# Split-product scores for the later pairs, first loads ahead of the branch, and a changed last sum and last stores in an attention and two-MLP kernel

## Chip, cores and metric

The kernel runs on one core of one Trainium2 chip. The metric is device microseconds of that core for one launch. Five engines run side by side, each through its own queue of instructions in order: PE (TensorE, matrix products; its weight loads are listed as PEld), DVE (VectorE), ACT (ScalarE), POOL (GpSimd) and SP (SyncE, which only issues DMAs here). They wait for one another through semaphores.

## Reference

```python
def _attn_ref(q, k, v, cap):                 # q, k, v: 4 x 12 x 448 x 64, cap = 30
    scores = scale * np.matmul(q, k.transpose(0, 1, 3, 2))
    scores = cap * np.tanh(scores / cap)
    scores = scores - np.max(scores, axis=-1, keepdims=True)
    attn = np.exp(scores)
    attn = attn / (np.sum(attn, axis=-1, keepdims=True) + 1e-09)
    return np.matmul(attn, v)
def _moe_ref(x, w_in, w_out):                # x: 1792 x 768, w_in: 768 x 2048
    h = np.maximum(x @ w_in, 0.0)
    return h * h @ w_out
def _moe2_ref(x, w_gate, w_val, w_out):      # 768 x 1536, twice; 1536 x 768
    g = x @ w_gate
    silu = g * (1.0 / (1.0 + np.exp(-g)))
    return silu * (x @ w_val) @ w_out
```

Attention over 4 batches and 12 heads gives 1792 rows of 768, and the two MLPs run on them one after the other.

## The kernel before

**Two programs and a branch.** `tile_capped_attention_moe_kernel` reads `cap` into a register on every engine (`values_load`, L1245) and branches (L1246). With a cap of at most 40 the program `arm(False, ...)` runs; `arm(True, ...)` is for larger caps and is not executed here. All loads stand behind the branch.

**Pairs.** Attention is worked through in 24 pairs of heads, 6 for each batch. A pair's k and q come in by DMA (`load_kq`), are transposed into a tile kT whose upper 64 partitions hold one head and lower 64 the other, and `scores` (L313 for early pairs, L323 for later ones) multiplies them: for every chunk c of 112 or 128 keys and each head j one matmul in plain fp32 with 64 rows of contraction and 448 columns. ACT applies tanh and exp, DVE adds up the sums, PE makes the row sums (`rs`) and the products with v (`av`, L443), DVE divides (`recip`, `norm`: tiles st, rc, rb, xs).

**Early and later pairs.** The first 12 pairs (batches 0 and 1) run one behind the other at the start. The other 12 are strewn over the first MLP's work for batches 0 and 1: four chunks of scores as two blocks of two chunks, with MLP matmuls between. Their results go to a buffer in DRAM (`xhold`), and the MLPs for batches 2 and 3 come after.

**MLPs.** An fp32 operand is split into `hi` (rounded to fp32r) and `lo` (the rest, fp32r too), and `mm3` (L592) replaces each product by three fp32r matmuls hi\*hi, lo\*hi, hi\*lo. In the first MLP's upper half the sums go straight on (relu, square); the other phases take products of blocks by a scheme with seven products for four blocks. Each down product is four such triples into one PSUM bank, and `d_gather` (L774, DVE) adds the bank to an accumulator `acc` in SBUF. At the end `out_tr` (L656, DVE) transposes `acc` into `ob`, and `out_store` (L669) issues four DMAs for two such tiles, all on SP.

**Order.** `Plan.order` sorts all steps by a table of costs and due times (`AHEAD`, `LATER`, with `ld` for the load, `tr` for the transposition, `sc` for the scores, and so on), and the code is written out in that order; at run time every engine follows it and waits for what isn't ready. Tiles of one tag share a ring of buffers (`r` two, `sg` two, `m` one).

Of the kernel before, what the change touches and what calls it, by code (L numbers as in the profile page):

```python
# [98 lines left out]


@with_exitstack
def arm(
    ctx: ExitStack,
    keep: bool,
    tc: tile.TileContext,
    q: bass.AP,
    k: bass.AP,
    v: bass.AP,
    cap: bass.AP,
    w_in: bass.AP,  # L110
# [19 lines left out]
    P = 128  # L130
# [47 lines left out]

    capt = const.tile([P, 4], F32, name="capt")
    ident = const.tile([P, P], F32, name="ident")  # L180
# [23 lines left out]
    def fine(b):  # L204
        return not keep and b < EARLY

    def load_kq(b, p):
        d = pair[b, p] = {}
        if rows(b, p) and fine(b):
            n = ap.tile([P, 2 * NC * D + S], F32, tag="kq", bufs=2, name="kq")  # L210
            d["k"] = n[:CP, : 2 * NC * D].rearrange("p (c j d) -> p c j d", j=2, d=D)
            d["q"] = n[:, 2 * NC * D :].rearrange("p (t d) -> p t d", d=32)
            nc.sync.dma_start(d["k"], k[b, 2 * p : 2 * p + 2].rearrange("j (p c) d -> p c j d", c=NC))
            for g in range(4):
                j, e = divmod(g, 2)
                nc.sync.dma_start(
                    d["q"][32 * g : 32 * g + 32],
                    q[b, 2 * p + j, :, 32 * e : 32 * e + 32].rearrange("(t r) d -> r t d", r=32),
                )
            return  # L220
        if rows(b, p):
            n = ap.tile([CP, 2, NC, 2, D], F32, tag="kq", bufs=2, name="kq")
            for i, src in enumerate((k, q)):
                nc.sync.dma_start(n[:, i], src[b, 2 * p : 2 * p + 2].rearrange("j (p c) d -> p c j d", c=NC))
        else:
            n = ap.tile([P, 2, TB, 32], F32, tag="kq", bufs=2, name="kq")
            for i, src in enumerate((k, q)):
                for g in range(4):
                    j, e = divmod(g, 2)
                    (nc.scalar if i and b < EARLY else nc.sync).dma_start(  # L230
                        n[32 * g : 32 * g + 32, i],
                        src[b, 2 * p + j, :, 32 * e : 32 * e + 32].rearrange("(t r) d -> r t d", r=32),
                    )
        d["n"] = n
# [55 lines left out]
    def tr_v(b, p, i):  # L290
# [282 lines left out]
    def w_lo(i):  # L573
        hi, lo = pieces[i]
        V.tensor_tensor(lo, raws[i], f32(hi), ALU.subtract)

    ffn_ps, g_t, r_t, tmp_t, acc_t, ob_t = {}, {}, {}, {}, {}, {}

# [28 lines left out]
    def relu(i, b):  # L607
        r_t[i, b] = fp.tile([P, S], F32, tag="r", bufs=2, name="r")
# [13 lines left out]
    def gate_t(i, b):  # L622
        r_t[i, b] = fp.tile([P, S], F32, tag="r", bufs=2, name="th")
        A.activation(r_t[i, b], ffn_ps[i, b], AF.Tanh, scale=0.5)
# [28 lines left out]
    def out_tr(b, m):  # L653
        if m % 2 == 0:
            ob_t[b, m // 2] = ap.tile([P, TB, 2, 32], F32, tag="mx", bufs=2, name="ob")
        V.transpose(out=ob_t[b, m // 2][:, :, m % 2], in_=acc_slice(b, m).rearrange("p (t r) -> p t r", r=32))  # L656

    def out_store(b, n):
        for i in range(4):
            c0 = 192 * i + 64 * n  # L660
            src = ob_t[b, n][32 * i : 32 * i + 32]
            if b < EARLY:
                nc.sync.dma_start(
                    out[b * S : (b + 1) * S, c0 : c0 + 64].rearrange("(t r) e -> r t e", r=32),
                    src.rearrange("p t m e -> p t (m e)"),
                )
            else:
                to = out[EARLY * S :, c0 : c0 + 64].rearrange("(t h r) e -> h r t e", h=2, r=32)
                nc.sync.dma_start(to[b - EARLY], src.rearrange("p t m e -> p t (m e)"))  # L669

# [46 lines left out]
    def q_mm(n, k, c, tag):  # L717
# [4 lines left out]
        mm3(qps[n, to], w[:, 0, c], w[:, 1, c], qx[x, c], first and c == 0, c == KH - 1)  # L722

    def d_mm(n, j, b, f0, c, tag):
        if c == 0:
            ffn_ps[n, j, b] = bank(tag)
        hi, lo = pieces[n, j]
        mm3(ffn_ps[n, j, b], hi[:, c], lo[:, c], g_t[b, f0 + c], c == 0, c == FG - 1)

# [4 lines left out]
    def part_add(n, to, name, k, tag):  # L734
        t = part[n, k] = fp.tile([P, S], F32, tag=tag, bufs=2, name="cb")
        V.tensor_tensor(t, qps[n, to], part.pop((n, name)), ALU.add)

    def q_relu(n, k):
        if k == "C21":
            part[n, k] = fp.tile([P, S], F32, tag="r", bufs=2, name="cb")  # L740
        A.activation(part[n, k], qps[n, "Z"] if k == "C21" else part[n, k], AF.Relu)
# [4 lines left out]
    def q_tanh(n, k):  # L746
        t = part[n, k, "th"] = fp.tile([P, S], F32, tag="r", bufs=2, name="th")
        A.activation(t, qps[n, "Z"] if k == "C21" else part[n, k], AF.Tanh, scale=0.5)
# [69 lines left out]
    def plan_pair(n, at, gate=()):  # L818
# [7 lines left out]
        before = [("ld", n - 1)] if n else []  # L826
        add(K("ld"), "SP", (1.8, 1.6) if n == 0 else (1.3, 2.0) if early and keep else (2.3, 3.6) if early else (3.2, 1.5), R("ld"), load_kq, (b, p),
            before + list(gate), [("kq", 2, [K("tr", 0), K("tr", 1)])])
        add(K("lv"), "SP", (1.4 if fine(b) else 0.5, 0.7), R("lv"), load_v, (b, p), [K("ld")], [("v", 2, [K("av", 3) if steps_av else K("av")])])
        tk = ("kT", 2, [K("sc", 3), K("sc", 2)] if early else [K("sc", 2)])  # L830
        if rows(b, p):
# [10 lines left out]
        else:  # L842
            for i in range(2):
                add(K("tr", i), "DVE", 0.64, R("tr"), tr_v, (b, p, i), [K("ld")] + [K("tr", 0)] * i, [] if i else [tk])
            src = [K("tr", 0), K("tr", 1)]
        line = (0, 1, 3, 2) if fine(b) else (0, 1, 2, 3)
        for c in line:
# [9 lines left out]
            elif c % 2 == 0:  # L857
                add(K("sc", c), "PE", 1.55, R("sc", c), lambda b, p, c: (scores(b, p, c), scores(b, p, c + 1)), (b, p, c),
                    src + ([K("sc", c - 2)] if c else [("av", n - 1)] if n > EARLY * KD else []), [("s", 1, [K("th", c)]), ("a", 1, [K("th", c + 1)])], pe)
# [44 lines left out]

    PAIR = 6.64
    steps = []
# [161 lines left out]

    end_of = {"kq": ("tr", B * KD - 1, 1), "kT": ("sc", B * KD - 1, 2), "m": ("sub", B * KD - 1, 3) if keep else ("ex", B * KD - 1, 3), "t": ("av", B * KD - 1)}

# [62 lines left out]
    for n, kk, b, t in seq:  # L1133
        u = items[n]
        K = lambda name, *a: (name, n, *a)
        if not ups(u):
            g, e, L = u[1], u[2][kk], u[0][0]
            tag = f"f{turn % 2}"
            turn += 1
            end = t + MM3 * FG  # L1140
            for c in range(FG):
                deps = [("pl", n, kk)] if c == 0 else [mm_key(n, kk, b, c - 1)]
                deps.append(("gl", b, L, FG * g + c))
                if c == 0:
                    deps.append(prev)
                add(mm_key(n, kk, b, c), "PE", MM3, t + MM3 * c, d_mm, (n, kk, b, FG * g, c, tag), deps,
                    [(tag, 2, [K("ga", kk, b)])] if c == 0 else [], MARGIN)
            prev = mm_key(n, kk, b, FG - 1)
# [9 lines left out]
            add(K("ga", kk, b), "DVE" if g else "ACT", DVE1 if g else ACT1, end, d_gather, (n, kk, b, e, g == 0), deps, ring)  # L1158
            if g == last(u) and L == "1":
# [73 lines left out]
    with tc.manual_schedule():  # L1233
        V.memset(zero, 0.0)
        make_identity(nc, ident)
        nc.sync.dma_start(capt[:, 0:1], cap[None, :].to_broadcast([P, 1]))
        G.memset(ones, 1.0)
# [5 lines left out]
def kernel(tc, q, k, v, cap, *rest):  # L1243
    nc = tc.nc
    rv = nc.values_load(cap[None, :].bitcast(I32), skip_runtime_bounds_check_because="only compared")  # L1245
    with tc.If((rv & 0x7FFFFFFF) <= 0x42200000) as cmp:  # L1246
        arm(False, tc, q, k, v, cap, *rest)
    with cmp.Else():
        arm(True, tc, q, k, v, cap, *rest)

# [29 lines left out]
```

## Time and profile before

| | |
|---|---|
| three runs, median | 1171.94 us (1166.28 to 1172.71) |
| profiled execution, its own time | 1168.75 us |
| span of its profile | 1166.9 us |
| PE busy | 1147.8 us (98%) |
| DVE busy | 882.8 us (76%) |
| ACT busy | 593.2 us (51%) |
| mean granted TensorE clock | 0.996 |

The span runs from the first to the last instruction; 1.85 us of the execution lie outside it. Matmuls are pipelined and a record's end is modelled, so a PE that is busy all the time need not be at its best: what a matmul costs is read from the distance between starts, or from the time that a row of many takes divided by their number. One fp32 matmul leaves two records, each with a weight load of its own; one fp32r matmul leaves one.

### The profile page before, as it was taken

To read this page: it belongs to the slowest core of one execution; us is meant where nothing else is said; L and a number is where in the kernel's file an instruction comes from. 1 tells how busy PE (TensorE), PEld (TensorE's weight loads), DVE (VectorE), ACT (ScalarE), POOL (GpSimd) and SP (SyncE) were. 2 spreads that over 40 slices of the span, in tenths; PEclk is the share of its full clock that TensorE was granted. 3 is DMA by queue.
4 is the path that set the end of the run, shared out by engine and by line. 5 is a ranking of instruction groups with operands and counts; after the bars stand their busy time and mean duration, and the time that the engine had idled before them with its cause. 6 is when DMAs were issued, how large, how long until landed. Compare 5 with 4: busy or idle time off the path is not lost.

```text
span 1166.9 us, 15975 instructions
## 1 busy us (share of the span) xinstructions
PE 1147.8 (98%) x5768; PEld 934.6 (80%) x5768; DVE 882.8 (76%) x1598; ACT 593.2 (51%) x1012; POOL 0.8 (0%) x7
## 2 busy tenths in 40 slices
PE   8999999999999999999999999999999999999997
PEld 5334767667767788999999999999989999999996
DVE  3799676677579679677787899589898995575764
ACT  5886365645643755563536654343254553541540
POOL 0000000000000000000000000000000000000000
PEclk9999999999999999999999999999999999999999
DMA  5653367455556574556455836555648252111214
GB/s 91 138 129 102 94 167 193 121 149 166 128 138 186 156 242 154 191 177 196 122 187 183 313 118 174 153 175 185 194 126 269 74 141 91 55 54 54 73 40 94
DMA packets 250385, 169.05 MB, mean 145 GB/s; under 512 B 167097, under 2 KB 222393, under 8 KB 250297
## 3 DMA queue, kind: packets, MB, share of 16 engines
q1 hardware_dynamic: 234904, 135.47, 41.7%
q10 hardware_dynamic: 15392, 32.48, 7.6%
q8 instruction: 47, 0.77, 0.3%
q14 instruction: 42, 0.34, 0.1%
HBM read 127.40 MB, written 40.50 MB: 144 GB/s over the span
## 4 chain that ended last, share of the span: by engine, by line
PE 87%; DVE 6%; DMA 3%; ACT 2%; issue 1%; SPq 0%; ACTq 0%; DVEq 0%
PE ff L592 73%; PE av L443 6%; PE sc L313 3%; PE sc L323 3%; DMA wr<-in_moe_w_out_dram 1%; PE rs L410 1%; DMA w<-wx 1%; DVE sm L400 1%; DVE wx L556 0%; DMA x<-xhold 0%; ACT tt L350 0%; PE rs L421 0%; DVE wq L707 0%; DVE wx L554 0%; SPq L539 0%
## 5 line engine op out<-in xcount | busy, mean ns | idle before, releaser
L592 PE MATMUL ff<-g,wd 128*128 128x448 f32 x1440 | 296.9, 367 | 0.0
L592 PEld LDWEIGHTS ff<-g,wd 128*128 128x128 f32 x1440 | 270.4, 188 | 24.9
L592 PE MATMUL ff<-x,wq 128*128 128x448 f32 x1152 | 246.4, 367 | 0.0
L592 PEld LDWEIGHTS ff<-x,wq 128*128 128x128 f32 x1152 | 216.3, 188 | 19.7
L592 PE MATMUL ff<-xq,wq 128*128 128x448 f32 x864 | 187.6, 367 | 1.3 <-DVE acc L648 1.3
L592 PEld LDWEIGHTS ff<-xq,wq 128*128 128x128 f32 x864 | 162.0, 188 | 17.1 <-ACT p L732 1.6
L592 PEld LDWEIGHTS ff<-g,wp 128*128 128x128 f32 x576 | 106.7, 188 | 25.1 <-issue 11.6
L592 PE MATMUL ff<-g,wp 128*128 128x448 f32 x576 | 123.5, 371 | 3.0 <-DVE g L640 2.0
L592 PEld LDWEIGHTS ff<-x,wp 128*128 128x128 f32 x576 | 106.3, 188 | 23.5 <-issue 14.2
L592 PE MATMUL ff<-x,wp 128*128 128x448 f32 x576 | 123.7, 370 | 0.0
L703 ACT CAST wq<-ws 128x384 fp32r<-128x384 f32 x128 | 64.8, 514 | 69.7 <-PE ff L592 39.6
L707 DVE TENSOR_TENSOR wq<-ws,wq 128x384 fp32r<-128x384 f32 x128 | 69.5, 552 | 33.1 <-ACT wq L703 32.6
L774 DVE TENSOR_TENSOR acc<-ff,acc 128x448 f32<-128x448 f32 x84 | 51.9, 620 | 36.7 <-PE ff L592 36.4
L703 ACT CAST wq<-wj 128x384 fp32r<-128x384 f32 x96 | 47.7, 511 | 59.2 <-PE ff L592 46.8
L556 DVE SCALAR_TENSOR_TENSOR wx<-wr,wx 128x512 int32<-128x512 int32 (+1 forms) x82 | 67.2, 819 | 2.0
L558 DVE SCALAR_TENSOR_TENSOR wx<-wr,wx 128x512 int32<-128x512 int32 (+1 forms) x82 | 67.0, 818 | 1.5
L763 ACT CAST g<-cb 128x448 fp32r<-128x448 f32 x80 | 45.2, 567 | 43.2 <-DVE cb L758 42.2
L554 DVE TENSOR_SCALAR wx<-wr 128x512 int32<-128x512 int32 (+1 forms) x82 | 39.9, 487 | 32.6 <-DMA w<-wx 16.6
L707 DVE TENSOR_TENSOR wq<-wj,wq 128x384 fp32r<-128x384 f32 x96 | 52.0, 549 | 16.1 <-ACT wq L703 16.1
L378 ACT ACTIVATE tt<-tt,capt 112x896 f32<-112x896 f32 (+1 forms) x60 | 59.8, 1040 | 0.1
L715 DVE TENSOR_TENSOR wd<-wj,wd 128x512 fp32r<-128x512 f32 x60 | 41.0, 684 | 24.6 <-ACT wd L711 24.6
L732 ACT COPY p<-ff 128x448 f32<-128x448 f32 x64 | 34.1, 532 | 44.2 <-PE ff L592 44.0
(91 smaller groups left out, 1223.4 us busy)
## 6 DMA issues: line engine op xcount, KB each, us to landing
wj<-w SPq DMA_DIRECT2D x64, 384.0 KB, 4.3
w<-wx ACTq DMA_DIRECT2D x40, 384.0 KB, 4.1
wj<-w SPq DMA_DIRECT2D x60, 256.0 KB, 2.9
wr<-in_moe_w_in_dram SPq DMA_DIRECT2D x16, 768.0 KB, 5.5
wr<-in_moe_w_out_dram SPq DMA_DIRECT2D x24, 512.0 KB, 4.3
w<-wx ACTq DMA_DIRECT2D x42, 256.0 KB, 2.3
wr<-in_moe_w_gate_dram SPq DMA_DIRECT2D x12, 768.0 KB, 5.7
wr<-in_moe_w_val_dram SPq DMA_DIRECT2D x12, 768.0 KB, 5.7
```

The costliest lines, as they stand in the source:

```text
L313: PE.matmul(ps[r] if c == 3 else ps[:, j], d["kT"][r, 0, c * P : min(c * P + P, S)], d["kT"][r, 1], start=True, stop=True)
L378: A.activation(t, t, AF.Exp, scale=capt[:, 1:2] if fine(b) else c_abs)
L443: PE.matmul(d["av"][64 * j : 64 * j + 64, :S], w, x, start=(c == 0), stop=(c == NC - 1),)
L554: V.tensor_scalar(x, hi, 3, 0x3FFFFFF8, ALU.logical_shift_left, ALU.bitwise_and)
L556: V.scalar_tensor_tensor(x, hi, -0x40000000, x, ALU.bitwise_and, ALU.bitwise_or)
L558: V.scalar_tensor_tensor(x, lo, 29, x, ALU.logical_shift_right, ALU.bitwise_or)
L592: PE.matmul(to, w, x[:, t], start=first and s == 0, stop=final and s == 2, skip_group_check=True)
L703: A.copy(pieces[n, k][:, 0], a_blk(n, k))
L707: V.tensor_tensor(w[:, 1], a_blk(n, k), f32(w[:, 0]), ALU.subtract)
L715: V.tensor_tensor(lo, blk[n][:, j], f32(hi), ALU.subtract)
L763: A.copy(g_t[b, f][:, 0], part[n, k])
L774: V.tensor_tensor(acc_slice(b, e), pt, acc_slice(b, e), ALU.add)
```

## The change

1. **Scores of the later pairs.** kT is split once per pair: `split_hi` (ACT, one cast of 128x896 into `kh`) and `split_lo` (DVE, two subtractions of 128x448 into `kl`). `split_scores` then makes each chunk's scores as three fp32r matmuls per head, in the order hi\*hi of both heads, lo\*hi of both, hi\*lo of both. In the plan, `ld` and `tr` of later pairs come earlier, `kh` and `kl` get due times, a score block is put down with 1.35 us in place of 1.55, and a pair with 6.1 us in place of 6.64.
2. **First pair.** The k and q of pair 0 and `cap` are loaded ahead of the branch, into a tile `rr` and a tile `capt`: k and then `cap` issued on SP, q on ACT. The two halves of `rr` serve as the `r` ring afterwards (`r_tile`).
3. **Last sum.** For the very last down product, ACT copies `acc` into the PSUM bank ahead of the matmuls (`d_seed`), these add to it, and `out_tr` reads the bank; the last DVE addition is gone.
4. **Last stores.** Of the last four stores, two go out on ACT's queue.

```diff
+def load_pieces(k_queue, q_queue, to, k, q, b, p):
+    for g in range(4):
+        j, e = divmod(g, 2)
+        for queue, i, src in ((k_queue, 0, k), (q_queue, 1, q)):
+            queue.dma_start(
+                to[32 * g : 32 * g + 32, i],
+                src[b, 2 * p + j, :, 32 * e : 32 * e + 32].rearrange("(t r) d -> r t d", r=32),
+            )
...
-            ld=-12.0, lv=-8.0, tr=-4.0, sc=0.0, th=2.0, ex=5.0, tot=8.0, av=13.0, rc=15.0, norm=18.0, xh=19.0, xl=20.0,
+            ld=-14.0, lv=-8.0, tr=-7.0, kh=-5.0, kl=-4.0, sc=0.0, th=2.0, ex=5.0, tot=8.0, av=13.0, rc=15.0, norm=18.0, xh=19.0, xl=20.0,
...
+    def split_hi(b, p):
+        d = pair[b, p]
+        d["hi"] = ap.tile([P, 2, S], F32R, tag="m", bufs=1, name="kh")
+        A.copy(d["hi"], d["kT"])
+
+    def split_lo(b, p, i):
+        d = pair[b, p]
+        d["lo", i] = fp.tile([P, S], F32R, tag="sg", bufs=2, name="kl")
+        V.tensor_tensor(d["lo", i], d["kT"][:, i], f32(d["hi"][:, i]), ALU.subtract)
+
+    def split_scores(b, p, c):
+        d = pair[b, p]
+        ps = d["s", c] = wide_bank(sc_tag(b, p, c), "sc")[:CP, :, :S]
+        col = slice(c * CP, (c + 1) * CP)
+        hi, lo = [d["hi"][:, i] for i in range(2)], [d["lo", i] for i in range(2)]
+        for s, (w, x) in enumerate(((hi[0], hi[1]), (lo[0], hi[1]), (hi[0], lo[1]))):
+            for j in range(2):
+                r = slice(64 * j, 64 * j + 64)
+                PE.matmul(ps[:, j], w[r, col], x[r], start=s == 0, stop=s == 2, skip_group_check=True)
...
+        src = ffn_ps.pop(("seed", b, m), None)
+        src = acc_slice(b, m) if src is None else src
...
+        final = b == EARLY and n == KH - 1
         for i in range(4):
+            queue = nc.scalar if final and i % 2 else nc.sync
...
+    def d_seed(n, j, b, e, tag):
+        ffn_ps[n, j, b] = ffn_ps["seed", b, e] = bank(tag)
+        A.copy(ffn_ps[n, j, b], acc_slice(b, e))
...
-    PAIR = 6.64
+    PAIR = 6.64 if keep else 6.1
...
+        with tc.manual_schedule():
+            load_pieces(nc.sync, nc.scalar, rr.rearrange("p i (t d) -> p i t d", d=32), k, q, 0, 0)
+            nc.sync.dma_start(capt[:, 0:1], cap[None, :].to_broadcast([128, 1]))
+        rv = nc.values_load(cap[None, :].bitcast(I32), skip_runtime_bounds_check_because="only compared")
```

PE at the first score block of the first later pair, before; sc is the score bank, kT the transposed k and q, ff an MLP bank, x and wp its operands:

```order
L592 MATMUL ff<-x_4_107,wp 128x448 x3
L323 MATMUL sc<-kT 112x448 x4
L592 MATMUL ff<-x_5_108,wp 128x448 x3
L592 MATMUL ff<-g,wp 128x448 x15
L410 MATMUL rs<-sm,ones 32x224 x4
```

and at the first block of the same pair after (kh and kl are the split halves of kT):

```order
L321 MATMUL sc<-kh 112x448 x2
L321 MATMUL sc<-kh,kl 112x448 x2
L321 MATMUL sc<-kl,kh 112x448 x2
L321 MATMUL sc<-kh 112x448 x2
L321 MATMUL sc<-kh,kl 112x448 x2
L321 MATMUL sc<-kl,kh 112x448 x2
L624 MATMUL ff<-x_5_118,wp 128x448 x3
```

Four matmuls in fp32 (two chunks, two heads) became twelve in fp32r; the MLP products around them stayed.

DVE around the end of the early pairs, before; xs and x are a pair's result and its split, st, rc and rb belong to the division, wp and wx to weights:

```order
L294 STREAM_TRANSPOSE kT<-kq 128x448 x2
L636 CAST g<-gg 128x448
L640 TENSOR_TENSOR g<-gg,g 128x448
L575 TENSOR_TENSOR wp<-wx,wp 128x768
L460 STREAM_TRANSPOSE st<-rs 128x224
L465 TENSOR_SCALAR rc<-st 128x14
L468 TENSOR_SCALAR rc<-st 32x7 x4
L472 RECIPROCAL rc<-rc 128x14
L475 STREAM_TRANSPOSE rb<-rc 128x448
L484 TENSOR_TENSOR xs<-av,rb 128x448
L554 TENSOR_SCALAR wx<-wr 128x512
```

and after:

```order
L672 TENSOR_TENSOR g<-gg,g 128x448
L311 TENSOR_TENSOR kl<-kT,kh 128x448
L486 STREAM_TRANSPOSE st<-rs 128x224
L491 TENSOR_SCALAR rc<-st 128x14
L494 TENSOR_SCALAR rc<-st 32x7 x4
L498 RECIPROCAL rc<-rc 128x14
L501 STREAM_TRANSPOSE rb<-rc 128x448
L510 TENSOR_TENSOR xs<-av,rb 128x448
L311 TENSOR_TENSOR kl<-kT,kh 128x448
L601 TENSOR_TENSOR wp<-wx,wp 128x768
```

The two subtractions stand on both sides of a division, ahead of a weight split that stood there before.

SP's queue from its start, before; kq and v are the loads of a pair, capt the cap:

```order
L1245 TENSOR_LOAD in_cap_dram_ptr
L1245 TENSOR_LOAD in_cap_dram
L1246 REGISTER_ALU
L1246 COMPARE_AND_BRANCH
L1236 DMA capt<-in_cap_dram 128x1
L230 DMA kq<-in_k_dram 32x14x32 x4
L213 DMA kq<-in_k_dram 112x8x64
```

and after, with the semaphores that the rows wait for:

```order
L105 DMA rr_58<-in_k_dram 32x14x32 x4
L1307 DMA capt_59<-in_cap_dram 128x1 [waits DMAHW0_49]
L1308 TENSOR_LOAD in_cap_dram_ptr
L1308 TENSOR_LOAD in_cap_dram
L1309 REGISTER_ALU
L1309 COMPARE_AND_BRANCH
L223 DMA kq_148<-in_k_dram 112x8x64 [waits DMAHW1_49]
```

The k loads went ahead of the branch; the load of cap went behind them and waits for a DMA semaphore (eight serve in turn, and this one is that of the first q load).

## Rows read from the trace of the kernel before

**Rows 1.** The page: busy time of each engine, chain by engine.

```profile
PE 1147.8 (98%) x5768; PEld 934.6 (80%) x5768; DVE 882.8 (76%) x1598; ACT 593.2 (51%) x1012; POOL 0.8 (0%) x7
PE 87%; DVE 6%; DMA 3%; ACT 2%; issue 1%; SPq 0%; ACTq 0%; DVEq 0%
```

**Rows 2.** Busy time of each engine in stretches: early pairs, a stall, later pairs.

```profile
core 0: us, PE busy (x) PEld busy (x) DVE busy (x) ACT busy (x) POOL busy (x), PEclk, DMA share, GB/s
60.00:70.00 10.00, 10.00 (x62) 3.45 (x60) 9.34 (x19) 7.44 (x10) 0.00 (x0) 1.00 0.50 94
...
150.00:160.00 10.00, 8.26 (x38) 3.79 (x36) 7.62 (x12) 5.59 (x10) 0.00 (x0) 0.83 0.45 100
...
160.00:416.00 256.00, 253.72 (x1275) 183.05 (x1273) 183.87 (x322) 144.35 (x199) 0.00 (x0) 1.00 0.59 161
```

**Rows 3.** Chain that ended last: start, us, what; later pairs and the MLP.

```profile
165.31 1.69 PE sc L323 x8
167.00 3.24 PE ff L592 x15
...
451.73 385.25 PE ff L592 x1863
```

**Rows 4.** Matmuls and weight loads by shape: busy us, mean ns of one.

```profile
L592 PE MATMUL ff<-g,wd 128*128 128x448 f32 x1440 | 296.9, 367 | 0.0
L592 PEld LDWEIGHTS ff<-g,wd 128*128 128x128 f32 x1440 | 270.4, 188 | 24.9
...
L323 PE MATMUL sc<-kT 64*112 64x448 f32 x192 | 42.3, 559 | 1.1 <-DVE xs L484 1.1
...
L323 PEld LDWEIGHTS sc<-kT 64*112 64x112 f32 x192 | 15.2, 172 | 18.0 <-issue 9.8 <-ACT tt L378 3.3 <-DVE xs L484 2.4
```

**Rows 5.** Timeline of weight loads at one score block: start, us, count.

```profile
165.71 0.18 PEld L323 LDWEIGHTS sc<-kT 64*112 64x112 f32 x2 [0.20 <-issue]
```

**Rows 6.** By shape, ACT and DVE: what a split like the new ones takes.

```profile
L378 ACT ACTIVATE tt<-tt,capt 112x896 f32<-112x896 f32 x48 | 47.4, 1041 | 0.0
...
L493 DVE TENSOR_TENSOR x<-x 128x448 fp32r<-128x448 f32 x27 | 16.4, 614 | 0.0
```

**Rows 7.** Timeline of the start, by engine: issues, cap, first transposition.

```profile
2.44 2.00 ACTq L230 DMA_DIRECT2D kq<-in_q_dram  x4
2.47 0.40 SPq L1236 DMA_DIRECT2D capt<-in_cap_dram  x1
...
2.92 3.07 SPq L230 DMA_DIRECT2D kq<-in_k_dram  x4
...
5.37 0.15 DVE L190 TENSOR_SCALAR capt<-capt 128x1 f32<-128x1 f32 x1 [2.64 <-DMA capt<-in_cap_dram]
...
5.95 0.15 DVE L193 TENSOR_SCALAR capt<-capt 128x1 f32<-128x1 f32 x1
...
8.18 1.17 DVE L294 STREAM_TRANSPOSE kT<-kq 128x448 f32<-128x448 f32 x2 [2.08 <-DMA kq<-in_k_dram]
```

**Rows 8.** Chain that ended last, at the start.

```profile
0.73 0.88 ACTq L1245
...
2.44 3.23 DMA kq<-in_q_dram
...
5.68 2.47 DMA kq<-in_k_dram
```

**Rows 9.** Timeline of ACT in the early pairs: start, us; idle before in brackets.

```profile
25.35 1.01 ACT L338 ACTIVATE tt<-sc,capt 128x896 f32<-128x896 f32 x1 [2.10 <-PE sc L313]
```

**Rows 10.** Timeline of the end: last DVE steps, last four stores.

```profile
1159.08 0.62 DVE L774 TENSOR_TENSOR acc<-ff,acc 128x448 f32<-128x448 f32 x1 [1.13 <-PE ff L592]
1159.74 0.65 DVE L656 STREAM_TRANSPOSE ob<-acc 128x448 f32<-128x448 f32 x1
...
1160.41 2.01 SPq L669 DMA_DIRECT2D out_dram<-ob  x4
```

**Rows 11.** DMA from 1160.4 to 1164.5 us: packets, MB, share of 16 engines.

```profile
q1 hardware_dynamic: 1856, 0.46, 50.0%
```

More of the change, by code (lines that the diff above doesn't have):

```diff
@@ L108, in arm @@
     v: bass.AP,
-    cap: bass.AP,
     w_in: bass.AP,
@@ L225, in load_kq @@
         else:
[L226 to L233, printed above, removed]
+            if b * KD + p:
+                n = ap.tile([P, 2, TB, 32], F32, tag="kq", bufs=2, name="kq")
+                load_pieces(nc.sync, nc.sync, n, k, q, b, p)
+            else:
+                n = rr.rearrange("p i (t d) -> p i t d", d=32)
         d["n"] = n
@@ L734, in part_add @@
     def part_add(n, to, name, k, tag):
-        t = part[n, k] = fp.tile([P, S], F32, tag=tag, bufs=2, name="cb")
+        t = part[n, k] = r_tile() if tag == "r" else fp.tile([P, S], F32, tag=tag, bufs=2, name="cb")
         V.tensor_tensor(t, qps[n, to], part.pop((n, name)), ALU.add)
@@ L845, in plan_pair @@
             src = [K("tr", 0), K("tr", 1)]
+        if not early and not keep:
+            add(K("kh"), "ACT", ACT2, R("kh"), split_hi, (b, p), src, [("m", 1, [K("sc", 2)])])
+            for i in range(2):
+                add(K("kl", i), "DVE", DVE1, R("kl", 0.7 * i), split_lo, (b, p, i), [K("kh")], [("sg", 2, [K("sc", 2)])])
+            src = [K("kl", 0), K("kl", 1)]
         line = (0, 1, 3, 2) if fine(b) else (0, 1, 2, 3)
@@ L857, in plan_pair @@
             elif c % 2 == 0:
[L858 removed]
+                one = scores if keep else split_scores
+                add(K("sc", c), "PE", 1.55 if keep else 1.35, R("sc", c), lambda b, p, c, one=one: (one(b, p, c), one(b, p, c + 1)), (b, p, c),
                     src + ([K("sc", c - 2)] if c else [("av", n - 1)] if n > EARLY * KD else []), [("s", 1, [K("th", c)]), ("a", 1, [K("th", c + 1)])], pe)
@@ L1140, in arm @@
             end = t + MM3 * FG
+            seeded = (n, kk, b, t) == seq[-1]
+            bank_of = [(tag, 2, [K("ga", kk, b)])]
+            if seeded:
+                bank_of = [(tag, 2, [("otr", b, e)])]
+                m = next(m for m, w in enumerate(items) if w[0] == u[0] and w[1] == g - 1 and w[2] == u[2] and w[3] == u[3])
+                add(K("sd", kk, b), "ACT", ACT1, t - 4.0, d_seed, (n, kk, b, e, tag), [("ga", m, kk, b), mm_key(n, kk, b + 1, 0)], bank_of)
             for c in range(FG):
                 deps = [("pl", n, kk)] if c == 0 else [mm_key(n, kk, b, c - 1)]
+                if seeded and c == 0:
+                    deps.append(K("sd", kk, b))
                 deps.append(("gl", b, L, FG * g + c))
@@ L1146, in arm @@
                 add(mm_key(n, kk, b, c), "PE", MM3, t + MM3 * c, d_mm, (n, kk, b, FG * g, c, tag), deps,
-                    [(tag, 2, [K("ga", kk, b)])] if c == 0 else [], MARGIN)
+                    bank_of if c == 0 and not seeded else [], MARGIN)
             prev = mm_key(n, kk, b, FG - 1)
@@ L1157, in arm @@
                 deps.append(("ga", m, kk, b))
-            add(K("ga", kk, b), "DVE" if g else "ACT", DVE1 if g else ACT1, end, d_gather, (n, kk, b, e, g == 0), deps, ring)
+            if seeded:
+                add(K("ga", kk, b), "DVE", 0.0, end, lambda: None, (), deps)
+            else:
+                add(K("ga", kk, b), "DVE" if g else "ACT", DVE1 if g else ACT1, end, d_gather, (n, kk, b, e, g == 0), deps, ring)
             if g == last(u) and L == "1":
```

45 lines of the change are left out of this document (26 added, 19 removed).

## Prediction

> **What bounds the kernel now.** I read the page first. PE is busy for 98% of the span and holds 87% of the chain that ended last; DVE comes next with 76% of the span and 6% of the chain [rows 1]. So a microsecond taken off PE's work counts where PE runs without a break, and work that is added elsewhere is free as long as PE doesn't wait for it. Then I read the stages. Among the early pairs DVE is full beside PE (9.34 of 10 us); once, at 150 to 160 us, PE starves (8.26) and the granted clock falls to 0.83; between 160 and 416 us, where ten of the twelve later pairs' scores lie, PE is busy for 253.7 of 256 us, DVE for 183.9 and ACT for 144.4 [rows 2]. There the chain is MLP products with score blocks between, and after 452 us a single piece of 385 us of MLP products [rows 3]. So the scores of the later pairs are bound by PE. At the start the chain is two register loads, the branch, and then DMA until DVE can transpose the first pair [rows 7, 8]; at the end it is one DVE addition, one transposition and four stores in a row [rows 10].
>
> **The change part by part: the scores.** A score block (two chunks, two heads) takes 1.69 us for eight records [rows 3], and there are 192 / 8 = 24 blocks [rows 4]. A record lasts 559 ns; an fp32r record with the same 448 columns lasts 367 [rows 4]. [...] They take 1.69, and two weight loads of 172 ns each stand within 0.18 us [rows 4, 5]: the two heads, in the upper and the lower 64 rows of the array, run at the same time. [...]
>
> After the change a block is six steps of one fp32r matmul per head. No row shows fp32r on half of the rows, so a step is bounded. [...] From above, still with two at a time, it is the distance of MLP products, 385.25 / 1863 = 0.207 us [rows 3]: 1.44 us, 0.25 less. In the MLP the load of 128 columns takes 188 ns, which nearly fills the step; loads of 112 columns take 172 [rows 4]. So I take 0.195 us: 1.37 us, 0.32 less, and 24 x 0.32 = **-7.7 us** (-6.0 to -8.9). What it would be without the overlap of the heads is a rival below.
>
> **Splitting kT.** Per later pair ACT gets a cast of 128x896, about 1.04 us (an activation of that length takes 1041 ns), and DVE two subtractions of 614 ns [rows 6]: 12.5 us more for ACT and 14.7 us for DVE in all. Between 160 and 416 us ACT has 112 us and DVE 72 us of idle time [rows 2]; that is the cover, and the transposition is put earlier in the plan to make room. Without cover a pair's first block would wait 1.04 + 1.23 us. The cover isn't whole: once PE's scores waited 1.1 us for DVE's xs [rows 4], at a place where DVE worked without a break, and there the two subtractions now stand in DVE's queue around the division that gives xs. I put **+1.0 us** for one such place (0 to +4). A gain isn't excluded either, since the stall at 150 to 160 us comes out of ACT's order, which changes a little; I leave it in the range. Tiles kh and kl take buffers of rings that these stages leave empty.
>
> **The first loads.** The first issues are at 2.44 us on ACT and 2.92 on SP, and DVE transposes at 8.18 [rows 7]. Now they are issued when the register load stood, at 0.73 us [rows 8], which looks like 1.7 us won. But cap is issued behind k and waits for the semaphore of the first q load, and DVE works on cap ahead of its transposition. The first q load took 3.23 us [rows 8]: 0.73 + 3.23 = 3.96. From issue to use cap took 5.37 - 2.47 = 2.90 us, and its four small steps 0.73 [rows 7]: 3.96 + 2.90 + 0.73 = 7.59 us against 8.18, or -0.6. If cap lands as fast as the last k load, in 2.47 us [rows 8], it is -1.0; if it has to queue behind the eight loads, nothing is won; if the first q lands sooner on an idle queue, up to -1.5. I take -0.8. Behind cap on SP stand the register loads, the branch and pair 1's loads: 3.96 + 0.40 for the issue + 1.7 for load and branch is 6.1, where pair 1's loads begin now (2.92 + 3.07 = 6.0) [rows 7], so they don't come later. Then the order: pair 1's third score chunk, for which ACT sat idle 2.10 us [rows 9], now stands ahead of pair 0's sums on PE, with the transposition of pair 2. PE's work is the same, but ACT gets its input sooner; I take -0.7 (0 to -1.2). Both stay won only if the full DVE behind them moves along; its order is the same from the fourth pair on. Together **-1.5 us** (0 to -2.7).
>
> **The end.** The DVE addition stood from 1159.08 to 1159.74 on the chain [rows 10]; ACT's copy into the bank lies under the 24 matmuls ahead of it. That is -0.66 us. The four stores are issued within 2.01 us on SP [rows 10]; two and two make it 1.0. But their 1856 packets hold 16 engines for half of 4.1 us, 2.05 us [rows 11], and now spread over about 3 us. So the second queue can win at most 0.9 us; I take -0.55 (0 to -0.9). Together **-1.2 us** (-0.66 to -1.6). [...]
>
> **The sum** against the profiled execution: 1168.75 - 7.7 + 1.0 - 1.5 - 1.2 = 1159.35 us. That execution lies 3.2 us under the median of the three and 2.5 over the lowest, so the median of new runs may well lie above the sum; I forecast **1160.5 us**.
>
> **Rivals.**
> A, the slower side: fp32r matmuls on half of the rows do not run two at a time. Only fp32 shows it in this trace. [...] Against it: the weight loads and matmuls of both heads start together in fp32, and the rows and banks used are the same.
> B: the splits are not covered. Every pair's two subtractions push something that PE waits for by a part of 1.23 us. Wholly exposed this is +14.7 and gives 1173; half, 1166; the change is worth nothing from 0.87 us per pair on ((7.7 + 2.7) / 12). For it: DVE is full among the early pairs and waits are short; against it: 72 us of idle DVE.
> [...]
> D: the loads ahead of the branch win nothing, because cap comes last; +0.8 on the forecast, within its range.
>
> **How the numbers follow.** Forecast with D 0.72, A 0.10, B 0.15, C 0.03. The forecast's own range is 1154 to 1166: all terms at their good ends give 1154.6 on the profiled execution, and the poor ends 1166. To hold 8 in 10, the range reaches into B, to 1170; A, C, the top of B and a little below 1154 stay out. 0.5% of the median, about what a measurement here can tell from no change, is 5.9 us, so faster means below 1166.1. Faster: 0.70 of the forecast and 0.04 of B, 0.74. Within 0.5%: 0.02 and 0.07, 0.09. Slower: A, C and 0.04 of B, 0.17.
>
> **What would show it.** [...] No new wait of the scores for kl or kh, and waits for xs no longer than now; else B. The first transposition at about 7.4 us, released by cap and not by k. The last transposition reading PSUM directly behind the last matmul, and about 1.2 us less from there to the end. Wrong would also be a stall at 150 to 160 us that grows, since the clock falls there.

## Result and profile after

The changed kernel takes 1153.9 us in the median of four runs (1153.39 to 1159.48), the kernel before 1170.44 in four runs beside them: a ratio of 0.987 (95% interval 0.983 to 0.992). It is faster by more than 0.5%, as forecast, and 0.1 us under the low end of the range. The profiled execution took 1153.43 us, against 1168.75 before and 1159.35 in the sum. The page of the changed kernel, beside [rows 1]:

```profile
span 1151.6 us, 16209 instructions
PE 1133.4 (98%) x5864; PEld 941.6 (82%) x5864; DVE 894.2 (78%) x1621; ACT 603.1 (52%) x1025; POOL 0.8 (0%) x7
PE 87%; DVE 5%; DMA 4%; ACT 2%; issue 1%; SPq 0%; DVEq 0%; ACTq 0%
q8 instruction: 48, 0.79, 0.3%
```

PE bounds the kernel as before. The spans differ by 15.2 us, 5.8 more than the sum says. To see where, I took the same MLP product in both traces (there are 4608 in either) and compared when it starts:

| stretch | before | after | difference |
|---|---|---|---|
| from the span's start to the 1209th product | 461.51 | 449.64 | -11.9 |
| from there to the 3209th | 413.64 | 410.69 | -2.95 |
| from there to the last product | 283.52 | 283.52 | 0 |
| from there to the end of the span | 8.20 | 7.79 | -0.4 |

**A score block**, in the timeline of PE (start, us, operation, count, what ended the idle time before it):

```profile
163.72 0.78 PE L624 MATMUL ff<-g,wp 128*128 128x448 f32 x3
164.43 0.46 PE L321 MATMUL sc<-kh 64*112 64x448 f32 x2
164.74 0.36 PE L321 MATMUL sc<-kh,kl 64*112 64x448 f32 x2
164.94 0.36 PE L321 MATMUL sc<-kl,kh 64*112 64x448 f32 x2
165.14 0.36 PE L321 MATMUL sc<-kh 64*112 64x448 f32 x2
165.34 0.37 PE L321 MATMUL sc<-kh,kl 64*112 64x448 f32 x2
165.55 0.37 PE L321 MATMUL sc<-kl,kh 64*112 64x448 f32 x2
165.84 1.48 PE L624 MATMUL ff<-g,wp 128*128 128x448 f32 x6
```

The two heads run together, 0.20 us apart from one pair of records to the next; from the block's first record to the next MLP product it is 1.41 us in place of 1.69 [rows 3]: 24 x 0.28 = 6.7 us. All 24 blocks take 1.40 to 1.41 us.

**The distance of MLP products**, in 100 us each that PE fills without a break; the kernel before, then the changed one (the number behind x counts PE's records):

```profile
500.00:600.00 100.00, 100.00 (x486) 90.83 (x485) 74.69 (x129) 50.97 (x99) 0.00 (x0) 1.00 0.58 174
1000.00:1100.00 100.00, 100.00 (x495) 92.68 (x494) 67.66 (x124) 41.84 (x83) 0.00 (x0) 1.00 0.19 64
```

```profile
500.00:600.00 100.00, 100.00 (x496) 92.69 (x495) 78.42 (x134) 46.43 (x91) 0.00 (x0) 1.00 0.56 166
700.00:800.00 100.00, 100.00 (x496) 92.68 (x495) 78.66 (x138) 42.29 (x84) 0.00 (x0) 1.00 0.57 175
```

The same product takes 0.2067 us in some rows and 0.2027 in others, at a granted clock of 1.00 in both. A row is here a run of products that follow one another without a break; the longer distance is called the long step, the shorter the short one. Before, 1978 products from 452 to 861 us took the longer step; after, nearly all took the shorter. Over the trace the longer steps cost 8.1 us before and 0.9 after: 7.2 us of the 15.2 that no edit asked for. They weren't all kept. In the changed kernel PE waits where the second phase of the MLPs ends (timeline of PE):

```profile
827.60 3.91 PE L624 MATMUL ff<-x,wq 128*128 128x448 f32 x18 [1.30 <-ACT u L773]
832.47 2.09 PE L624 MATMUL ff<-xq,wq 128*128 128x448 f32 x9 [0.96 <-DVE cb L777]
...
846.44 2.09 PE L624 MATMUL ff<-xq,wq 128*128 128x448 f32 x9 [0.93 <-DVE rr L777]
```

What waited before and no longer does, in the timeline of PE of the kernel before:

```profile
152.48 0.67 PE L592 MATMUL ff<-g,wp 128*128 128x448 f32 x2 [0.94 <-ACT g L636]
153.96 1.25 PE L592 MATMUL ff<-g,wp 128*128 128x448 f32 x3 [0.81 <-DVE g L640]
...
190.49 1.01 PE L323 MATMUL sc<-kT 64*112 64x448 f32 x4 [1.05 <-DVE xs L484]
...
249.63 1.08 PE L592 MATMUL ff<-g,wp 128*128 128x448 f32 x4 [1.22 <-DVE g L640]
```

The last two are gone, of the first two 1.06 and 0.19 us are left, and the granted clock stays at 1.00 there (0.83 in [rows 2]).

### The profile page after: what moved, and what is told of

It reads as the page before. It is cut to its first block, busy times and chain, and to the rows that moved or that the text cites. A ratio compares the mean times of both kernels' runs of the same rounds, so it can differ in the third digit from the quotient of the medians.

```text
span 1151.6 us, 16209 instructions
## 1 busy us (share of the span) xinstructions
PE 1133.4 (98%) x5864; PEld 941.6 (82%) x5864; DVE 894.2 (78%) x1621; ACT 603.1 (52%) x1025; POOL 0.8 (0%) x7
## 4 chain that ended last, share of the span: by engine, by line
PE 87%; DVE 5%; DMA 4%; ACT 2%; issue 1%; SPq 0%; DVEq 0%; ACTq 0%
PE ff L624 71%; PE av L469 6%; PE sc L339 4%; PE sc L321 3%; DMA wr<-in_moe_w_val_dram 1%; PE rs L436 1%; DMA wr<-in_moe_w_out_dram 1%; PE warm L853 1%; DMA yhold<-acc 1%; DVE wq L743 1%; DVE wx L582 1%; DMA w<-wx 1%; PE rs L447 1%; DMA wr<-in_moe_w_gate_dram 0%; ACT tt L376 0%
## 5 line engine op out<-in xcount | busy, mean ns | idle before, releaser
L624 PE MATMUL ff<-g,wd 128*128 128x448 f32 x1440 | 293.5, 365 | 0.0
L624 PEld LDWEIGHTS ff<-g,wd 128*128 128x128 f32 x1440 | 270.5, 188 | 21.3
L580 DVE TENSOR_SCALAR wx<-wr 128x512 int32<-128x512 int32 (+1 forms) x82 | 39.9, 487 | 37.3 <-DMA wr<-in_moe_w_out_dram 20.0
L804 ACT CAST g<-cb 128x448 fp32r<-128x448 f32 x64 | 36.1, 567 | 43.4 <-DVE cb L799 43.0
L376 ACT ACTIVATE tt<-sc,capt 112x896 f32<-112x896 f32 x48 | 45.8, 1006 | 20.5 <-PE sc L321 20.5
```

Source lines behind the costliest of these rows:

```text
L376: A.activation(d["t", c], d.pop(("s", c)), AF.Tanh, scale=c_inv)
L580: V.tensor_scalar(x, hi, 3, 0x3FFFFFF8, ALU.logical_shift_left, ALU.bitwise_and)
L624: PE.matmul(to, w, x[:, t], start=first and s == 0, stop=final and s == 2, skip_group_check=True)
```

## Experiments

Theory 1: each part is worth what its own place shows, and the rest is the step of the product rows and waits that move. Rival: the plan's new order brought the rest.

**The kernel before once more.** No edit.

> The kernel before, unchanged, profiled a second time. In its first profile the MLP products stand 0.2067 us apart from 452 to 861 us (1978 in a row) and 0.2027 us apart nearly everywhere else; in the changed kernel nearly all stand 0.2027 apart. 1978 x 0.004 = 7.9 us, about half of the difference between the two profiles. Theory 1 (the distance is set anew wherever PE resumes after a break, by something that is no part of the change): the long stretch may come out at either distance, 1168 us with the longer, 1160 to 1161 with the shorter, and the distance changes only at breaks. Theory 2 (the distance belongs to the program, its tiles and their places): the same stretch again at 0.2067, and a time within 1 us of 1168.75.

1167.98 us median, 1169.10 in the profile (ratio 1.002, 0.9985 to 1.0049). Windows of its trace:

```profile
500.00:600.00 100.00, 100.00 (x495) 92.67 (x494) 76.52 (x131) 50.54 (x99) 0.00 (x0) 1.00 0.59 178
...
1000.00:1100.00 100.00, 100.00 (x486) 90.81 (x485) 67.10 (x123) 41.05 (x83) 0.00 (x0) 1.00 0.17 56
```

The other way round: short step from 452 to 670 us, long from 693 us to the end, 9.3 us in all. Theory 2 falls: the step isn't the program's. Theory 1 had the time wrong, since it thought of one stretch only; and the step doesn't change at visible breaks alone: here it did so 21 us behind one, without a wait to be seen. In seven of the fourteen profiles of this study a row changes like this, and each time at the same place, the 2349th product or the one behind it, where the products go over from the tile x to xq. In the four profiles whose row keeps the long step there, a few steps of 201 to 205 ns stand at this place among those of 206 to 207. So it looks like a break too small to show as a wait; what makes it, the profile doesn't say. The runs of the kernel before in this study reach from 1160.6 to 1173.6 us; long rows, at up to 12 us in one profile below, could account for nearly all of that width.

**The parts one by one.** Only the scores with their plan, only the first loads, only the end.

> The kernel before with the split scores alone, the plan's constants for them (ld, tr, kh, kl, a block of 1.35 us, a pair of 6.1 us) among it; first loads and end as before. Theory 1: each of 24 blocks takes 1.41 us in place of 1.69, -6.7 us, plus or minus 3 us for stalls that move (the one at 150 us, the waits for xs at 190 and 250 us, new ones around 830 to 846 us), plus or minus the 7.9 us of the long stretch: 1161 to 1163 us with MLP products at 0.2067 us from 452 to 861 us, 1153 to 1155 with them at 0.2027. Rival (the order of the plan and not the distance of products brought the rest): about 1156 whatever the distance.

> The kernel before with the first pair's loads and cap ahead of the branch alone (k and q into rr, whose halves then serve as the r ring). Theory 1: the first score at 7.7 us in place of 9.4, of which 1.4 us are still there at 140 us, and the stall at 150 us as before or moved; -1.4 us where the distance of products in the long stretch is the same as in the kernel before, -9.3 where it is the shorter one. Rival: the loads' gain is lost again at the stall at 150 us, which hangs on ACT's order and not on PE's; then 0.

> The kernel before with the last sum in PSUM and the last four stores on two queues alone. Theory 1: the DVE addition is gone (-0.66 us from the last matmul to the last transposition's end), the stores on two queues win nothing: 7.3 to 7.4 us from the end of the last matmul to the end of the span in place of 7.85, -0.5 us in all. Rival (what was forecast): -1.2 us. The total moves by these 0.5 to 1.2 us, or by 8 more where the long stretch of products has the shorter distance; all ahead of the last down product is the kernel before.

| | median, us | ratio (95%) | to the 1209th product | last product to end |
|---|---|---|---|---|
| before, both profiles | | | 461.51, 460.89 | 8.20, 8.25 |
| only scores | 1158.66 | 0.995 (0.992 to 0.998) | 452.20 | 8.18 |
| only first loads | 1164.75 | 0.999 (0.996 to 1.002) | 460.93 | 8.14 |
| only end | 1166.42 | 1.000 (0.998 to 1.003) | 460.95 | 7.76 |

The scores give 8.7 to 9.3 us up to the 1209th product. Their profile has the short step nearly throughout and came out at 1158.54, not at the 1153 to 1155 expected of it, since PE waits there late in the second phase; the timeline of PE:

```profile
831.12 3.91 PE L611 MATMUL ff<-x,wq 128*128 128x448 f32 x18 [1.28 <-ACT u L751]
836.15 2.09 PE L611 MATMUL ff<-xq,wq 128*128 128x448 f32 x9 [1.11 <-DVE cb L755]
...
850.87 2.10 PE L611 MATMUL ff<-xq,wq 128*128 128x448 f32 x9 [1.68 <-DVE cb L755]
```

The first loads were 1.0 us ahead at 140 us and 0 to 0.6 at the 1209th product (against the one or the other profile of the kernel before): nearer to the rival's 0 than to theory 1's 1.4. The end gave 0.44, near theory 1's 0.5 and far from the 1.2 forecast. A side result: the run with the end alone has the same two gaps at 152 us as the kernel before (0.94 and 0.80 us), yet in its windows a granted clock of 1.00 there:

```profile
150.00:160.00 10.00, 8.26 (x45) 4.54 (x44) 7.65 (x12) 5.54 (x10) 0.00 (x0) 1.00 0.43 106
```

So the half clock of [rows 2] is not a fixed cost of that stall. Between the same two products at 155 and 167 us the run with the end alone is 0.5 us shorter than the first profile of the kernel before; against the other two profiles in which the clock fell there it is 0.3 and 1.0 us.

**The plan alone.**

```diff
-            ld=-12.0, lv=-8.0, tr=-4.0, sc=0.0, th=2.0, ex=5.0, tot=8.0, av=13.0, rc=15.0, norm=18.0, xh=19.0, xl=20.0,
+            ld=-14.0, lv=-8.0, tr=-7.0, sc=0.0, th=2.0, ex=5.0, tot=8.0, av=13.0, rc=15.0, norm=18.0, xh=19.0, xl=20.0,
...
-                add(K("sc", c), "PE", 1.55, R("sc", c), lambda b, p, c: (scores(b, p, c), scores(b, p, c + 1)), (b, p, c),
+                add(K("sc", c), "PE", 1.55 if keep else 1.35, R("sc", c), lambda b, p, c: (scores(b, p, c), scores(b, p, c + 1)), (b, p, c),
...
-    PAIR = 6.64
+    PAIR = 6.64 if keep else 6.1
```

> The kernel before with the plan's constants of the change alone (later pairs' loads and transpositions earlier, a block counted 1.35 us, a pair 6.1 us), scores still in fp32 and without the splits. Theory 1 (the waits at 190 us, 1.05 us, and at 250 us, 1.22 us, went away because the plan puts the steps in another order): both are gone or below 0.3 us here too, and up to 452 us the kernel is 2 to 3 us ahead of the kernel before. Rival (they went away because shorter blocks shift PE against DVE): both stay, and the time up to 452 us is that of before within 0.7 us. The whole lies at 1158 to 1170 by the distance of products either way.

1167.25 us (0.999, 0.996 to 1.002). Timeline of PE:

```profile
246.87 1.07 PE L592 MATMUL ff<-g,wp 128*128 128x448 f32 x4 [1.20 <-DVE g L640]
...
337.85 0.68 PE L592 MATMUL ff<-g,wp 128*128 128x448 f32 x2 [2.15 <-ACT g L636]
```

The wait at 190 us and most of the second gap at 152 us are gone, so these belong to the order. The one at 250 us stays, a new one of 2.15 us stands at 338, and the 1209th product comes at 463.98, 2.5 us later than before. Neither theory holds whole: the order moves waits about, and only with the shorter blocks do they all go.

**Splits done twice.** The loop body of `split_lo` runs two times, 24 subtractions more.

> The changed kernel with each of the 24 DVE subtractions that make kl done twice (the same result): 24 x 0.61 = 14.7 us more on DVE between 124 and 383 us. Theory 1 (the splits lie under PE's work, and were worth 0 and not the 1.0 us forecast): PE's time from 140 to 450 us grows by less than 1.5 us. Rival (DVE's cover is used up, and the splits already cost something): 5 us or more, with scores waiting for kl or av's successors for xs.

1157.37 us (0.993, 0.990 to 0.996). Windows from the same product to the same product, changed kernel and this one:

```profile
140.00:450.00 310.00, 307.82 (x1665) 239.07 (x1664) 249.81 (x446) 190.67 (x276) 0.00 (x0) 1.00 0.60 170
```

```profile
141.11:451.00 309.89, 307.95 (x1665) 239.39 (x1664) 262.46 (x468) 190.58 (x276) 0.00 (x0) 1.00 0.60 170
```

DVE has 12.7 us more to do there, and PE's 1665 records take as long. DVE's cover takes as much again at no cost, so the subtractions that the change has can hardly cost anything: rival B is out. ACT's cast was not doubled; that it too is covered is read from the changed kernel alone, where no score waits for kh or kl.

**Breaks in the product rows.**

```diff
             qps[n, to] = bank(tag)
+            if to == "Z" and n % 2 == 0:
+                PE.matmul(qps[n, to][:16, :16], zero[:, :16], zero[:, :16], start=True, stop=True)
```

> The changed kernel with one matmul of 16x16 more ahead of every second group of seven products in the upper half's successors (16 places between 450 and 1090 us), into a bank that the next product overwrites: each is a break in the row of MLP products. Theory (which of the two steps, 0.2027 or 0.2067 us, a row of products takes is drawn anew at a break, with about 15% for the longer one, 68 of 442 rows so far): no row longer than some 190 products; short rows on either side of long ones; the longer step in 5 to 35% of the products behind 450 us, and not in none or in half or more of them as in most profiles so far; each break itself costs 0.1 to 0.3 us, 2 to 5 us in all. Rival (the step belongs to a stretch of time or of the program): the step stays the same across the breaks.

1156.3 to 1158.9 us in seven runs (0.992, 0.990 to 0.995). Windows inside three of its rows:

```profile
510.00:545.00 35.00, 35.00 (x171) 31.80 (x170) 27.36 (x47) 13.01 (x25) 0.00 (x0) 1.00 0.60 177
...
620.00:655.00 35.00, 35.00 (x174) 32.46 (x173) 27.88 (x49) 22.22 (x43) 0.00 (x0) 1.00 0.90 314
...
945.00:980.00 35.00, 35.00 (x171) 31.81 (x170) 19.95 (x37) 15.75 (x32) 0.00 (x0) 1.00 0.27 83
```

171, 174 and 171 records in 35 us: long rows stand between short ones, and 641 of the 3400 products behind 450 us (19%) are in long ones. In this profile every change of the step stands at a break or at the place near the 2349th product, so that the step is set anew at a break holds as far as one profile can show it; the rows are up to 331 products long, not 190, as some breaks lie closer than others. The runs lie within 2.6 us of one another, where eight runs of the splits done twice spread over 9.8. The breaks don't make the kernel faster: the median is 1157.17, against 1153.9 of the changed kernel.

**48 PE instructions more.**

```diff
         PE.matmul(warm_t[0][:, :P], zero, zero, start=True, stop=True)
+        if i == 16:
+            for _ in range(12):
+                PE.matmul(warm_t[0][:16, :16], zero[:, :16], zero[:, :16], start=True, stop=True)
```

> The changed kernel with 12 matmuls of 16x16 more at a place near 8 us where PE waits anyway: 48 PE instructions, nothing else. In the changed kernel two packets of the instruction queue (16 KB, 1.03 to 1.05 us on one DMA engine) fall at 796.3 and 820.6 us into loads of raw weights (7.35 us for one that takes 5.6 in the kernels without the split scores), DVE's splits come 1.7 and 1.3 us later, and PE waits 1.30, 0.96 and 0.93 us at 827, 832 and 846 us. [...] Theory: the load at 791 us takes 5.6 to 5.8 us, and the three waits together fall from 3.2 us to below 1.2. Rival (the loads are slow for another reason, such as the place of tiles or the higher pace of PE): the waits stay at 3 us or more.

1153.01 us (0.988, 0.983 to 0.993), span 1149.7. The changed kernel's chain at the first of these loads, and the DMA queues while it runs:

```profile
791.14 7.35 DMA wr<-in_moe_w_val_dram
798.51 0.57 DVE wx L580
```

```profile
q1 hardware_dynamic: 1065, 1.55, 57.2%
q10 hardware_dynamic: 144, 0.39, 12.2%
q8 instruction: 1, 0.02, 0.8%
```

Here, DVE and PE in the timeline, and the queues while the same load runs:

```profile
797.57 0.56 DVE L580 TENSOR_SCALAR wx<-wr 128x768 int32<-128x768 int32 x1 [0.81 <-DMA wr<-in_moe_w_val_dram]
...
843.88 2.09 PE L624 MATMUL ff<-xq,wq 128*128 128x448 f32 x9 [0.46 <-DVE rr L777]
```

```profile
q1 hardware_dynamic: 1072, 1.57, 58.7%
q10 hardware_dynamic: 144, 0.39, 13.0%
```

No packet of the instruction queue falls into the load; it is issued at 791.84, used at 797.57, so 5.7 us and not 7.35. The load that met the second packet, one of `w_out`, took 5.35 us from its issue to its use, and 6.6 in the changed kernel. Of 3.2 us of waits up to 850 us, 0.46 is left, and 0.65 stands at 857.6. The packets moved by 6.7 and 7.6 us, off the loads. They now stand 14.6 and 37.9 us behind the 2809th product, where they are in every kernel with fp32 scores (12.5 to 13.9 and 37.3 to 38.0); with the split scores and nothing added to PE's code they stand at 20.6 to 21.3 and 44.8 to 45.5. The other profiles agree. In the three with split scores whose packets were moved (this one, the breaks, and the three edits together below) PE waits 0.2 to 1.1 us in this stretch, in the six others 1.5 to 4.1. By its median this run can't be told from the changed kernel (1153.9). So by these profiles part of what the split scores win is lost, 3.2 us of waits up to 850 us against 0.46 here: their 96 PE records more (5864 for 5768), each with its weight load, put two code packets into loads of raw weights for which DVE stands waiting, with PE's work behind them in its queue.

**The start: fewer warm-ups, and the table early.**

```diff
-    GB, TBUF, WP, NPRE, NWARM = 8, 4, 8, 3, 30
+    GB, TBUF, WP, NPRE, NWARM = 8, 4, 8, 3, 25
...
         PE.matmul(warm_t[0][:, :P], zero, zero, start=True, stop=True)
+        if i == 16:
+            for _ in range(5):
+                PE.matmul(warm_t[0][:16, :16], zero[:, :16], zero[:, :16], start=True, stop=True)
...
```

```diff
         G.memset(ones, 1.0)
+        A.activation(capt[:, 3:4], zero[:, 0:1], AF.Tanh)
```

> The changed kernel with 11 in place of 14 warm-up matmuls ahead of the first scores (25 in place of 30 in all, and five small ones of 16x16 so that the number of PE instructions stays). In the changed kernel's profile the transpositions of pair 0 end at 7.65 us and the warm-ups at 7.72, and the first score starts at 7.71. The warm-ups take 0.213 us a record until the clock rises and 0.111 after, and it rose at 5.7 to 8.7 us in the profiles so far, so that the warm-ups ended at 7.55 to 8.97. Theory (with the loads ahead of the branch it is the warm-ups that end last): 22 records end by 7.5 us whatever the clock does, and the first score starts at 7.65 to 7.8 us. Rival (with fewer warm-ups the clock rises later and the first scores pay for it): the first score stands at 7.7, but the third block of scores ends later than in the changed kernel, by 1 us or more.

> The changed kernel with one tanh of 128x1 on ACT behind the branch, ahead of all else that ACT does there. In the changed kernel ACT waits for the first scores until 8.81 us, and only then loads its table (1.28 us), so that the first tanh runs at 10.11. Theory: the table is loaded at about 5.6 us, the first tanh runs at 8.85 us, and of these 1.26 us 0.8 to 1.2 are still there at 140 us, where PE's MLP products begin to fill the time. Rival (DVE is full behind it and holds the early pairs): less than 0.3 us is left at 140 us.

Timeline of the start, changed kernel; then two rows of the run with all last stores on SP, whose start is the same program:

```profile
2.76 4.96 PE L853 MATMUL warm<-zero 128*128 128x128 f32 x28 [2.76 <-DVE zero L1292]
...
5.71 0.15 DVE L200 TENSOR_SCALAR capt<-capt 128x1 f32<-128x1 f32 x1 [3.01 <-DMA capt<-in_cap_dram]
...
6.48 1.17 DVE L301 STREAM_TRANSPOSE kT<-rr 128x448 f32<-128x448 f32 x2
7.71 2.67 PE L339 MATMUL sc<-kT 64*128 64x448 f32 x12
...
8.81 1.28 ACT L364 ACT_TABLE_LOAD   x1 [8.81 <-PE sc L339]
```

```profile
2.76 6.04 PE L853 MATMUL warm<-zero 128*128 128x128 f32 x28 [2.76 <-DVE zero L1292]
...
8.73 2.30 PE L339 MATMUL sc<-kT 64*128 64x448 f32 x10
```

The transposition starts at 6.48 and 6.49 us, but the warm-ups end at 7.72 and 8.80: their records stand 0.213 us apart up to 6.1 us in the one and up to 8.4 in the other, and 0.111 from there on. That the clock rises there is my reading: the windows print a granted clock of 1.00 on either side, and the trace's own clock records begin at this place (6.08 us in the changed kernel, 7.48 in the kernel before). With fewer of them, in the same view:

```profile
2.77 4.91 PE L853 MATMUL warm<-zero 128*128 128x128 f32 x22 [2.77 <-DVE zero L1295]
...
7.83 2.67 PE L339 MATMUL sc<-kT 64*128 64x448 f32 x12 [0.15 <-DVE kT L301]
```

Now the transposition (7.78) ends last and the warm-ups end at 7.68, with the same 2.67 us for the first twelve records: the theory holds in kind, with both of its times missed by 0.2 us or less (7.5 for the warm-ups, 7.65 to 7.8 for the first score), and the rival does not. In the changed kernel's own profile there was nothing to win, in others up to 1.0 us; 1155.92 us in the median (0.990, 0.987 to 0.993) can't tell. With the early table the first tanh ran at 8.84 us in place of 10.11, 0.8 of it was left at 140 us, and by 680 us it was lost in a wait of 1.46 us at 661 us (0.54 in the changed kernel): 1155.24 us (0.989, 0.984 to 0.993), no gain on the changed kernel.

**The last stores on one queue.**

```diff
-            queue = nc.scalar if final and i % 2 else nc.sync
+            queue = nc.sync
```

> The changed kernel with all of the last four stores on SP. Theory 1 (the second queue wins nothing, since the second store of each queue takes 1.44 and 1.50 us to issue where on SP alone it takes 0.5): from the end of the last transposition to the end of the span 6.4 to 6.7 us, as the 6.5 of the kernel before, against 6.7 with two queues; so 0 to 0.3 us less. Rival (what was forecast: two queues win 0.55 us): 7.2 us.

Timelines of the end, the changed kernel and then this one:

```profile
1144.26 0.65 DVE L690 STREAM_TRANSPOSE ob<-ff 128x448 f32<-128x448 f32 x1 [1.12 <-PE ff L624]
1144.94 1.85 ACTq L705 DMA_DIRECT2D out_dram<-ob  x2
```

```profile
1155.63 0.65 DVE L690 STREAM_TRANSPOSE ob<-ff 128x448 f32<-128x448 f32 x1 [1.17 <-PE ff L624]
1156.30 2.49 SPq L705 DMA_DIRECT2D out_dram<-ob  x4
```

From the end of the last transposition to the end of the span it is 6.74 us with two queues and 6.72 with one, against 6.49 in the kernel before. The two queues save 0.6 us of issue against the one (1.86 us on SP and 1.85 on ACT, against 2.49) and nothing at the end: the rival falls. Theory 1's 6.4 to 6.7 is missed by a hair. The median of eight runs is 1157.30 (0.991, 0.988 to 0.995); this profile has the long step from 457 to 835 and from 947 us on, 12.2 us in all, and a span of 1163.0.

**Together.** The 48 instructions, the early table and 11 warm-ups ahead of the first scores.

> The changed kernel with the 48 PE instructions more (in all as many as in the run with them alone), the early table load and 11 warm-ups ahead of the first scores. Against the run with the 48 instructions alone (1149.7 us of span): the first tanh 1.3 to 2 us earlier, of which 0.8 to 1.5 are left at 140 us and behind it, since the weights behind 785 us no longer hold PE up: a span of 1148.2 to 1148.9 us where the long rows have the shorter step, and a median 2 to 4 us below that of the changed kernel. Rival (what is won early is waited for at the weights, as in the run with the early table alone): 1149.7 or more.

1149.7 to 1160.4 us in six runs, median 1155.38 (0.990, 0.986 to 0.994). The profile has 1845 products in one long row (chain: start, us, what), long steps of 8.6 us over the trace, and a span of 1155.9 us:

```profile
455.52 381.56 PE ff L624 x1845
```

So the 1148.2 to 1148.9 us expected for short steps was not seen in a profile. At 140 us it is 2.0 us ahead of the kernel before (the 48 instructions alone: 0.2), and its best run is the fastest of all. By the median it is no better than the changed kernel: how many rows draw the long step weighs more than all three edits. A version that is surely faster than both was not found.

## Why the prediction held, step by step

- **Scores, -7.7.** Right that the heads run two at a time, 1.0 too much in size: a step is 0.201 us, not 0.195, so -6.7. Beside six steps the 1.37 and the 1.44 us of a block hold 0.20 us for going over to the block's shape and back. No run shows that by itself, and none a step as short as the -8.9 of the range takes. The traces show, as medians over the 24 blocks: the pairs of records start 0.295, 0.202, 0.200, 0.202 and 0.202 us apart, and the next MLP product 0.302 behind the last pair, 1.41 in all, of which 0.19 are more than six steps; before, it was 0.467, 0.376 and 0.376, then 0.472, 1.69 in all. Rival A falls on these rows: the heads run two at a time, and 96 loads of 170 to 172 ns of each kind pass under 0.20 us steps on the same rows of the array.
- **Splits, +1.0.** Wrong in sign. The step that failed was to charge a wait at a place where DVE is full. The subtractions are covered twice over, and the waits at 190 and 250 us, 2.3 us, disappeared: the first by the order, the second only with order and blocks together. The gain was named as not excluded, and not priced.
- **Start, -1.5.** The transposition came 1.7 us earlier and not 0.8, released by cap as said: cap was used 2.6 us behind its issue at 3.11 us, which came before the 3.96 that I had set. But I didn't ask what is late next. It is the warm-ups: at 140 us the gain was 1.4 us in this profile and 0.2 to 1.0 in other runs with 14 of them and the table as it was. Of the 0.7 us for the order nothing is seen: the first MLP product came 1.77 us earlier, about as much as the first score (1.70). So the 1.4 is near the forecast by luck.
- **End, -1.2.** The addition gave 0.65: from the end of the last matmul to the end of the last transposition it is 0.69 us in place of 1.34. The stores gave +0.25 in place of -0.55. Issuing was not the bound; on each queue the second store took 1.44 and 1.50 us to issue, and with one queue the end is the same. Why the end behind the transposition is 0.25 longer than before stays open; the stores now follow those of the pair before by 4.2 us in place of 4.9, and whether the packets of those still hold the DMA engines was not shown.
- **The rest.** On the profiles: blocks -6.7, waits at 190 and 250 us -2.3, the stall at 152 us with its clock -1.0, start -1.4, end -0.4, the wait at the change of phases (1.27 to 0.74) -0.5, long steps -7.2, new waits from 660 us on +3.7; in sum -15.8 of the 15.2 measured, the remainder unassigned. So the forecast's own four terms gave -8.5 of its -9.4. The waits that went (-3.8) and the new ones (+3.7), neither of them priced, cancelled one another by luck. The distance between sum and profile is what the forecast took as fixed: one distance of products, 0.207 us, for the whole kernel. The same holds for the time that it started from: over the 28 runs of the kernel before beside the last experiments the median is 1166.2, not 1171.94, and against that the change is worth 12 us. That is still the changed kernel's four runs, of which three lie at 1153.4 to 1154.4; the run with the last stores on one queue, which differs from it in nothing else, has 1157.3 over eight runs, 9 us. With the long steps taken off, the two profiles are 8 us apart (1158.8 and 1150.7). That the median lies at the low end of the range is thus in part luck with the long rows.
- **Slips in the working.** The terms' good ends add up to 1155.5 us, not to the 1154.6 that the low end was taken from (1168.75 - 8.9 - 2.7 - 1.6). And eleven of the twelve later pairs have their scores between 160 and 416 us, not ten; nothing hangs on it.

## What to carry over

Here the split fp32 products paid (1.41 us a block for 1.69) where the work on two halves of the array already ran in pairs: a forecast counts the steps, here 0.20 us each, and the longer ones into and out of the block, here 0.30. Before a difference of under 1% is put down to an edit, count the records in stretches where an engine runs without a break, in both traces, and profile the unchanged kernel twice. When a start is shortened, list what ends just behind the thing removed; when instructions are added, look where the code packets now fall.

## What the runs showed of the hardware

- A row of equal fp32r products of 448 columns runs at 0.2027 or 0.2067 us a product, at the same granted clock, for up to 1978 products; 68 of the 442 rows in the first ten profiles took the longer. What decides it is open; in the one profile with added breaks each change stood at a break or near the 2349th product, and in seven of fourteen profiles it changed within a row, always there.
- The instruction queue q8, 48 packets of 16 KB (0.79 MB) in the changed kernel, stands in the page beside the data as a share of the same 16 DMA engines; 48 PE instructions more moved two of its packets by 6.7 and 7.6 us. One came for about 25 us of products, and each took 0.9 to 1.9 us of one engine. A load that met one took 7.35 us, where the next two took 5.6 to 5.7.
- At the same two gaps of 0.94 and 0.8 us at 152 us the clock fell to half for 3.4 us in three profiles and stayed in one; at the start the warm-ups went from 0.213 to 0.111 us a record between 5.7 and 8.7 us.
